# A new hand-written order of steps for a two-layer kernel (gated linear attention, then a leaky-ReLU feed-forward), on all engines and in the transfer queue

## The chip, the cores and the metric

One core of one Trainium2 chip runs the whole program. The metric is the device time of one execution in microseconds (us). The time of the kernel before the change is the median of three runs. One further execution was profiled; its trace is what the views below come from.

## The reference: what is computed

The inputs are q, k, v and f_logit, each of shape (4 batches, 8 heads, 768 steps, 48), and two weight matrices.

```
f = sigmoid(f_logit)
for t in range(768):
    state = f[t][:, None] * state + outer(k[t], v[t])      # per batch and head, 48 x 48
    y[t]  = q[t] @ state
x = y with heads side by side                               # 3072 tokens x 384
h = x @ w_in                                                # 384 -> 2048
out = maximum(0.01 * h, h) @ w_out                          # 2048 -> 384, float32
```

## The kernel before the change

The 768 steps are cut into six chunks of 128. The work is done in twelve units, numbered j = 0 to 11. Units 0 to 3 ("paired") take chunks 0 and 1 of one batch each; units 4 to 11 take one later chunk of two batches, two units for each chunk. Each unit yields 256 tokens, and the feed-forward part runs over these 256 tokens. Most steps exist twice for a unit, with a second number a = 0 or 1 (2 means both at once).

The program is one straight list of steps. Every step is a word in a long string called `order`; a word such as `dn_0_1_0@6` names a function, its numbers, and after the @ the PSUM banks that it writes. A loop at the end of the kernel (L659) splits each word and calls the function from a table called `parts`. The functions issue instructions to fixed engines, so the string at once sets the order in which each engine gets its work, and the order of the transfers, which all go through the queue of SyncE (SP in the profile). The engines run their own lists in order and wait for each other by semaphores.

The words, with the line at which their instructions show in the profile:

- **Transfers:** `Lf`, `Lk`, `Lq`, `Lv` load the inputs of a unit (384 KB for a paired unit at L158, two of 192 KB for a later one at L162). `WI_0` to `WI_4` load the pieces of w_in (L176; 384 KB for pieces 0 and 1, 768 KB for the other three) and `WO_0` to `WO_3` the quarters of w_out (768 KB, L181 and L184). The large pieces share three ring buffers, so WO_0 has to wait until piece WI_2 has been cast. `xk` and `xq` are transposing transfers of the scaled k and q for units 4 to 11 (L355), `ed` a small transfer of decays, `st` and `sh` store results.
- **Gates, on ScalarE (ACT):** `ge` and `gl` take an exponential and a logarithm of the gate (L236, L248); `cs` sums the logarithms over time on TensorE (L257 to L268); `dec` turns the sums into decays (L276 to L285).
- **Scaling:** `k` and `q` multiply by the decays (L301, on VectorE or GpSimd); for units 0 to 3 `tk` and `tq` transpose on TensorE (L335) and `ck`, `cq` copy the result out of PSUM (L348, L350).
- **Attention:** `sc` computes the scores (L371 for paired units, L378 for later ones), `mk` masks them on VectorE (L388, L392), `v` casts v (L307 to L316), `mx` and `ms` compute y (L409), `xt` copies it out as x (L469, L471). `pt`, `sf` and `sb` keep the running state (L482 to L508).
- **Feed-forward:** `cw` casts a half of a weight piece (L199 on ACT, L201 on VectorE or GpSimd). `up` is six matmuls of the first layer (L516) for a pair of 128-wide slices, `pr` the leaky ReLU on ACT (L521), `dn` four matmuls of the second layer (L528), `ob` the copy of the result out of PSUM. The last tile is done in two column halves, `dh`, `oh` and `sh` (L550 to L564).
- **Filling:** `id_n` issues matmuls of n times 128 columns on a constant tile (L207). Nothing reads their results; they keep TensorE busy where the list expects it to wait.

The last digit of `k`, `q`, `v`, `ck`, `cq`, `cw`, `xt`, `ob` and `sb` chooses the engine. Input buffers exist five times, PSUM has eight banks of 512 columns.

Of the kernel before, what the change touches and what calls it, by code (L numbers as in the profile page):

```python
# [15 lines left out]
def kernel(  # L16
# [587 lines left out]
    pr_1_3 WO_1 up_1_2@0 pr_1_0 Lf_3_2 cw_0_6_0 up_0_4@2 pr_1_2 cw_0_7_0 up_0_5@5 pr_0_4 WO_2 up_0_6@1 pr_0_5
    cw_1_0_0 cw_1_1_2 up_1_5@3 pr_0_6 up_1_7@4 pr_1_5 q_2_1_0 WO_3 up_1_4@6 pr_1_7 q_2_0_0 Lv_2_2 tq_2_1@7
    k_2_1_0 k_2_0_1 pr_1_4 Lq_3_2 dn_0_1_0@0 cq_2_1_0 Lf_4_1 tq_2_0@2 tk_2_1@5 Lf_4_0 cq_2_0_1 up_1_6@1 ck_2_1_0
    Lv_3_2 tk_2_0@3 cw_1_3_1 cw_1_2_2 dn_1_0_0@4 ck_2_0_0 pr_1_6 sc_2_1@6.7 sc_2_0@2.5 Lk_3_2 ge_3_0 mk_2_1_1
    dn_0_0_0@3 ge_3_1 mk_2_0_0 gl_3_0 dn_1_0_1 gl_3_1 mk_2_1_0 up_0_7@1 Lk_4_0 cw_1_4_1 cw_1_5_2 mk_2_0_1
    cs_3_0@7 pr_0_7 dn_0_1_1 dec_3_0 cs_3_1@2 Lf_5_1 cw_1_6_0 dn_0_0_1 dec_3_1 cw_1_7_0 dn_1_1_0@6 dn_0_0_2
    Lf_5_0 v_2_1_1 v_2_0_0 dn_1_1_1 dn_1_0_2 Lk_4_1 q_3_1_0 q_3_0_1 pt_2_2@5.1 mx_2_2@7.2 sf_2_0 Lv_4_1 dn_1_0_3  # L610
    xt_2_0_1 sb_2_0_1 tq_3_1@5 Lv_4_0 ge_4_2 sf_2_1 tq_3_0@7 dn_1_1_2 cq_3_1_0 sb_2_1_0 gl_4_2 ms_2 cq_3_0_0
    Lf_6_1 dn_1_1_3 ob_1_0_0 v_3_1_1 xt_2_1_0 dn_0_0_3 ob_1_1_1 Lf_6_0 k_3_1_0 k_3_0_1 v_3_0_1 cs_4_0@1 ob_0_0_0
    cs_4_1@5 dn_0_1_2 dec_4_0 Lq_4_0 tk_3_1@7 dn_0_1_3 dec_4_1 ck_3_1_0 Lq_4_1 tk_3_0@4 Lq_5_1 ge_5_2 ob_0_1_0
    up_2_0@2 ck_3_0_0 pt_3_2@6.3 pr_2_0 sc_3_0@1.7 sf_3_0 gl_5_2 Lk_5_0 sc_3_1@5.0 k_4_2_1 up_2_1@4 mk_3_1_0
    Lk_5_1 up_2_5@2 mk_3_0_1 pr_2_1 sb_3_0_0 up_2_2@6 mk_3_1_1 pr_2_5 Lq_5_0 up_2_4@5 v_4_2_0 mk_3_0_0 pr_2_2
    xk_4 sf_3_1 up_2_3@7 pr_2_4 dn_2_1_0@4 sb_3_1_1 pr_2_3 pt_4_1@0 ge_6_2 cs_5_1@2 cs_5_0@1 sf_4_1 up_2_7@6
    gl_6_2 sb_4_1_1 mx_3_2@3.5 q_4_2_1 pr_2_7 pt_4_0@7 xt_3_0_0 cs_6_0@0 dec_5_0 ms_3 sf_4_0 dn_2_0_0@6 xt_3_1_0
    cs_6_1@3 sb_4_0_0 dn_2_1_1 xq_4 dec_5_1 dn_2_0_1 k_5_2_0 st_0_1 up_3_3@7 dec_6_1 q_5_2_1 dn_2_1_2 pr_3_3
    up_2_6@5 dec_6_0 up_3_2@1 xq_5 pr_2_6 up_3_1@2 pr_3_2 up_3_0@3 pr_3_1 xk_5 dn_2_1_3 pr_3_0 up_3_7@7 Lv_5_0
    up_3_5@0 Lv_5_1 pr_3_7 ob_2_1_0 sc_4_2@5.1.2.3 Lf_7_0 pr_3_5 dn_3_0_0@7 Lf_7_1 mk_4_1_1 st_0_0 dn_2_0_2  # L620
    mk_4_0_1 ed_5 dn_3_0_1 mk_4_1_0 Lk_6_1 mk_4_0_0 dn_2_0_3 dn_3_1_0@4 Lk_6_0 up_3_4@0 Lv_6_1 sc_5_2@3.1.2.5
    pr_3_4 dn_3_1_1 Lv_6_0 v_5_2_0 mk_5_1_1 up_3_6@0 mk_5_0_1 st_1_1 dn_3_0_2 mk_5_1_0 pr_3_6 mk_5_0_0
    mx_4_2@5.1 st_1_0 ge_7_2 Lq_6_1 mx_5_2@2.0 gl_7_2 xt_4_1_0 Lf_8_1 xt_4_0_0 ob_2_0_1 pt_5_1@3 pt_5_0@1
    xt_5_0_1 dn_3_1_2 sf_5_1 Lf_8_0 xt_5_1_1 sf_5_0 up_4_0@5 sb_5_1_0 Lq_6_0 dn_3_0_3 sb_5_0_1 pr_4_0 cs_7_0@6
    cs_7_1@2 Lv_7_1 dn_3_1_3 dec_7_0 k_6_2_0 up_5_5@3 Lv_7_0 v_6_2_0 up_4_1@0 Lq_7_0 ob_3_1_0 pr_5_5 Lq_7_1
    ob_3_0_0 up_4_2@1 dec_7_1 up_5_0@5 Lk_7_0 pt_6_0@6 pt_6_1@4 up_5_1@3 sf_6_0 pr_4_1 Lk_7_1 pr_5_0 sf_6_1
    up_5_3@7 pr_5_1 xk_6 sb_6_0_1 dn_4_0_0@2 sb_6_1_0 pr_4_2 pr_5_3 up_5_2@0 q_6_2_0 ge_8_2 dn_5_1_0@6 pr_5_2
    up_4_7@5 gl_8_2 up_5_4@4 v_7_2_0 xq_6 pr_4_7 up_4_3@3 pr_5_4 cs_8_0@1 pr_4_3 st_3_1 cs_8_1@7 dn_4_1_0@0
# [5 lines left out]
    mk_7_1_0 gl_9_2 Lq_9_0 up_6_4@2 sf_7_0 ob_5_0_1 mx_7_2@6.1 ob_4_1_0 Lq_9_1 pr_6_1 sb_7_0_0 sf_7_1 pr_6_4
    up_6_5@4 xt_7_0_1 xt_7_1_0 sb_7_1_0 up_6_7@5 k_8_2_0 pr_6_5 up_7_5@0 pr_6_7 v_8_2_0 up_7_6@3 pr_7_5 up_6_0@2
    pr_7_6 q_8_2_0 cs_9_1@7 cs_9_0@6 pr_6_0 up_7_0@1 dec_9_1 dn_6_0_0@4 xq_8 up_7_4@5 pr_7_0 up_7_1@0 pr_7_4
    xk_8 dn_6_1_0@3 pr_7_1 up_7_2@2 dec_9_0 Lf_10_1 k_9_2_1 dn_7_1_0@7 Lf_10_0 q_9_2_0 up_6_6@1 st_5_1 pr_7_2
    up_7_3@5 pr_6_6 dn_7_0_0@0 pr_7_3 xq_9 up_7_7@6 dn_7_1_1 pr_7_7 st_5_0 up_6_3@2 xk_9 dn_7_0_1 pr_6_3
    dn_7_1_2 Lv_9_0 ge_10_2 sc_8_2@1.5.6.2 Lv_9_1 dn_7_0_2 st_4_0 mk_8_0_1 gl_10_2 Lf_11_1 dn_7_1_3 mk_8_1_0
    ed_9 pt_8_1@5 mk_8_1_1 dn_7_0_3 ob_7_1_1 Lf_11_0 sf_8_1 dn_6_1_1 ob_7_0_1 st_4_1 mk_8_0_0 sb_8_1_0 dn_6_0_1  # L640
    dn_6_1_2 dn_6_0_2 Lq_10_1 dn_6_1_3 mx_8_2@6.2 Lq_10_0 sc_9_2@7.5.0.1 xt_8_1_1 xt_8_0_0 Lk_10_1 v_9_2_0
    dn_6_0_3 mk_9_0_0 Lk_10_0 cs_10_0@2 mk_9_1_0 pt_8_0@6 up_8_0@7 dec_10_0 Lq_11_1 sf_8_0 up_8_3@0 Lq_11_0
    ob_6_0_1 mk_9_1_1 sb_8_0_0 pr_8_0 Lk_11_1 cs_10_1@2 pt_9_0@6 mk_9_0_1 pt_9_1@4 pr_8_3 Lk_11_0 up_8_1@1
    sf_9_1 dec_10_1 up_8_4@7 ob_6_1_0 Lv_10_1 sb_9_1_0 pr_8_1 up_8_2@5 sf_9_0 ge_11_2 Lv_10_0 dn_8_0_0@0
    q_10_2_0 pr_8_4 sb_9_0_0 up_8_6@4 gl_11_2 st_6_0 mx_9_2@2.3 pr_8_6 xq_10 pr_8_2 cs_11_0@1 xt_9_0_0 cs_11_1@6
    k_10_2_1 dn_8_1_0@7 dec_11_0 xt_9_1_0 dn_8_0_1 dec_11_1 dn_8_1_1 xk_10 q_11_2_1 up_8_5@4 up_9_4@5 pr_8_5
    up_8_7@2 pr_9_4 xq_11 k_11_2_1 dn_8_0_2 pr_8_7 up_9_0@3 st_7_0 dn_8_0_3 pr_9_0 xk_11 v_10_2_0 dn_8_1_2
    ob_8_0_0 up_9_1@1 st_7_1 Lv_11_1 up_9_3@6 pr_9_1 Lv_11_0 up_9_2@4 pr_9_3 st_6_1 dn_9_1_0@5 pr_9_2 dn_9_0_0@2
    up_9_7@3 st_8_0 up_9_5@0 pr_9_7 dn_9_0_1 pr_9_5 up_9_6@1 sc_10_2@6.4.3.0 pr_9_6 dn_9_1_1 mk_10_1_0 dn_9_0_2
    mk_10_0_1 dn_9_1_2 mk_10_1_1 mk_10_0_0 dn_9_0_3 dn_9_1_3 ob_9_0_0 mx_10_2@1.3 ob_9_1_0 sc_11_2@4.0.6.2  # L650
    xt_10_1_1 xt_10_0_0 v_11_2_0 dn_8_1_3 mk_11_1_0 up_10_4@5 mk_11_1_1 ob_8_1_1 up_10_6@1 mk_11_0_1 st_8_1
    pr_10_4 st_9_1 mk_11_0_0 up_10_0@3 pr_10_6 st_9_0 up_10_1@6 pr_10_0 up_10_2@2 pr_10_1 up_10_3@7 pr_10_2
    up_10_7@0 pr_10_3 mx_11_2@5.4 pr_10_7 dn_10_1_0@1 xt_11_0_1 xt_11_1_0 up_10_5@3 dn_10_1_1 pr_10_5 up_11_6@6
# [39 lines left out]
```

## Time and profile before

| | |
|---|---|
| time, median of 3 runs (lowest to highest) | 178.56 us (177.96 to 178.77) |
| the profiled execution, time and span | 178.35 us and 176.6 us |
| TensorE busy (PE) | 170.0 us, 96% of the span |
| ScalarE, VectorE, GpSimd busy | 119.7, 89.3 and 55.9 us |
| transfers | 34.44 MB, mean 195 GB/s |

The span runs from the first to the last instruction that the profile shows; the time has 1.75 us around it. PE is TensorE's matmuls, PEld its weight loads, DVE is VectorE, POOL is GpSimd, and SPq is the queue of SyncE that issues the transfers. In the groups, the columns are line, engine, operation, output and inputs, shapes, count, then busy time in us and the mean of one in ns, then the engine's idle time before these instructions and what ended it.

### The profile page before, as it was taken

How to read it: one execution, taken by the hardware profiler on the slowest of the kernel's cores; microseconds unless marked ns; L12 is line 12 of the kernel's file. 1: busy time of each engine (PE TensorE's matmuls, PEld its weight loads, DVE VectorE, ACT ScalarE, POOL GpSimd, SP SyncE). 2: the span in 40 equal slices, each digit the busy share in tenths (PEclk: the TensorE clock that was granted, in tenths of full speed). 3: DMA queues.
4: the chain of work that ended last, by engine and by line, in shares of the span. 5: the costliest groups of instructions: out<-in, count | busy, mean ns of one | idle time of the engine just before them, and what ended most of it. 6: DMA issues, size and time to landing. Idle time of an engine off the chain costs nothing.

```text
span 176.6 us, 5545 instructions
## 1 busy us (share of the span) xinstructions
PE 170.0 (96%) x2295; PEld 129.7 (73%) x2295; DVE 89.3 (51%) x194; ACT 119.7 (68%) x244; POOL 55.9 (32%) x103
## 2 busy tenths in 40 slices
...
GB/s 139 282 301 262 344 341 339 388 296 219 185 198 193 166 182 162 171 214 206 169 203 207 213 182 183 189 242 205 190 170 208 196 222 112 137 4 0 0 71 111
DMA packets 106856, 34.44 MB, mean 195 GB/s; under 512 B 101072, under 2 KB 105040, under 8 KB 106832
## 3 DMA queue, kind: packets, MB, share of 16 engines
...
## 4 chain that ended last, share of the span: by engine, by line
PE 71%; SPq 14%; DMA 10%; POOL 1%; issue 1%; DVE 1%; ACT 0%; DVEq 0%
PE ps L516 30%; PE ps L528 29%; SPq L158 9%; PE ps L409 5%; DMA ring<-in_moe_w_in_dram 4%; DMA k_raw<-in_k_dram 3%; DMA ring<-in_moe_w_out_dram 3%; SPq L162 3%; SPq L176 3%; PE ps L378 3%; PE ps L550 2%; PE ps L265 1%; PE ps L487 1%; POOL w_out L201 1%; ACT w_in L199 0%
## 5 line engine op out<-in xcount | busy, mean ns | idle before, releaser
L516 PE MATMUL ps<-xT,w_in 128*128 128x256 bf16 x576 | 70.0, 273 | 0.7 <-ACT w_in L199 0.7
L521 ACT ACTIVATE gT<-ps 128x512 bf16<-128x512 f32 x96 | 55.6, 610 | 21.6 <-PE ps L516 19.3
L528 PE MATMUL ps<-w_out,gT 128*128 128x384 bf16 x368 | 68.4, 326 | 0.0
L516 PEld LDWEIGHTS <-w_in 128*128 128x128 bf16 x576 | 60.8, 110 | 6.2 <-ACT w_in L199 0.9
L528 PEld LDWEIGHTS <-gT 128*128 128x128 bf16 x368 | 34.2, 98 | 19.1
L392 DVE TENSOR_TENSOR wm<-ps,ut 128x512 bf16<-128x512 f32 x32 | 20.1, 684 | 14.0 <-ACT gT L521 8.0
L307 POOL CAST vb<-v_raw 128x768 bf16<-128x768 f32 (+1 forms) x11 | 8.1, 738 | 31.7 <-DMA v_raw<-in_v_dram 29.1
L505 POOL TENSOR_TENSOR sf<-sf,end 128x192 f32<-128x192 f32 x12 | 6.9, 571 | 31.3 <-DVE sf L499 27.5
L301 POOL TENSOR_TENSOR kh<-k_raw,em 128x768 bf16<-128x768 f32 (+1 forms) x8 | 11.7, 1458 | 12.8 <-DMA k_raw<-in_k_dram 6.7
L301 DVE TENSOR_TENSOR qh<-q_raw,at 128x384 bf16<-128x384 f32 (+1 forms) x11 | 9.2, 845 | 11.4 <-DMA q_raw<-in_q_dram 7.8
L574 DVE COPY osb<-ps 128x384 f32<-128x384 f32 x12 | 6.6, 556 | 15.0 <-PE ps L528 13.5
L276 ACT ACTIVATE em<-ps 128x384 bf16<-128x384 f32 x24 | 12.1, 503 | 2.0 <-PE ps L265 1.2
L469 ACT CAST xT<-ps 128x384 bf16<-128x384 f32 x11 | 5.6, 534 | 11.1 <-PE ps L409 11.0
L236 ACT ACTIVATE f_raw<-f_raw 128x384 f32<-128x384 f32 (+1 forms) x16 | 10.8, 689 | 3.1 <-DMA f_raw<-in_f_logit_dram 2.9
L508 POOL CAST sb<-sf 64x192 bf16<-64x192 f32 x30 | 11.3, 376 | 3.6 <-DVE sf L497 1.9
L471 DVE CAST xT<-ps 128x384 bf16<-128x384 f32 x13 | 7.2, 567 | 10.1 <-PE ps L409 10.0
L277 ACT ACTIVATE at<-ps 128x384 bf16<-128x384 f32 x24 | 12.2, 508 | 0.0
L499 DVE TENSOR_TENSOR sf<-sf,ps 64x192 f32<-64x192 f32 x32 | 11.2, 351 | 0.7
L207 PE MATMUL ps<-warm 128*128 128x512 bf16 (+3 forms) x31 | 10.2, 441 | 1.1 <-DVE warm L83 1.1
L388 DVE TENSOR_TENSOR wm<-ps,pair_mask 128x512 bf16<-128x512 f32 x16 | 10.1, 686 | 1.9 <-PE ps L371 1.8
L248 ACT ACTIVATE lf<-f_raw 128x384 bf16<-128x384 f32 (+1 forms) x16 | 10.7, 687 | 0.2
L572 ACT COPY osb<-ps 128x384 f32<-128x384 f32 x11 | 5.3, 479 | 8.1 <-PE ps L528 8.0
...
## 6 DMA issues: line engine op xcount, KB each, us to landing
...
```

The costliest lines, as they stand in the source:

```text
L158: nc.sync.dma_start(out=by_pair(raw(j, x))[:, h].rearrange("t h s d -> t h (s d)"), in_=srcs[x][j, h, 0:2 * C, :].rearrange("h (t s) d -> ...
L236: nc.scalar.activation(gates(j)[:, part], gates(j)[:, part], AF.Exp, scale=-1.0)
L248: nc.scalar.activation(dst, src, AF.Ln, bias=1.0)
L276: nc.scalar.activation(ems[j % 2][:, a], t[:, 0:H * D], AF.Exp, scale=1.0)
L277: nc.scalar.activation(ats[j % 2][:, a], t[:, 0:H * D], AF.Exp, scale=-1.0)
L301: eng.tensor_mul(heads(j, to[j % NR], a)[:, :, :, 0:D], raw_heads(j, x, a), decays(j, by, a))
L392: nc.vector.tensor_mul(w, src.rearrange("t (p n) -> t p n", p=P2), ut[:, None, :].to_broadcast([128, P2, 128]))
L499: nc.vector.tensor_add(sf[rows], sf[rows], new)
L508: eng.tensor_copy(out=sb[rows, :, y * D:y * D + D], in_=sf[rows])
L516: nc.tensor.matmul(pm[:, i, :], w_in_of(ff, kk), xTs[j % 3][:, kk].rearrange("t a s -> t (a s)"), start=(kk == 0), stop=(kk == NK - 1))
L521: nc.scalar.activation(gTs[j % 3][:, 2 * g:2 * g + 2, :], pm, AF.Prelu, alpha=0.01)
L528: nc.tensor.matmul(po, gTs[j % 3][:, ff, 128 * a:128 * a + 128], w_out_b[quarter][:, ff % 4, :], start=(ff == 0), stop=(ff == NF - 1))
```

## The change

Only the string `order` changes. Apart from the filling and the digit that chooses an engine, the same steps are there, each once. TensorE's list, the lists of the other engines and the list of transfers are all in a new order, and many PSUM banks are others. The filling goes from 112 times 128 columns in twelve places to 102 in nine. Some copies, casts and scalings go to another engine: ACT copies 9 `xt` and 9 `ob` in place of 11 and 11, and 5 `ck` in place of 2, VectorE the others; the casts of weights are 6 on ACT, 4 on VectorE and 6 on GpSimd in place of 4, 7 and 5.

Among the transfers, Lf_2 and Lv_1 come before WI_1, Lk_2 comes before WO_0, and Lk_3 comes before WO_3, Lq_3, Lv_3 and the two Lf_4. Lf_7 comes before unit 5's transposes and Lf_6 after unit 4's; Lk_7 and Lv_7 come after unit 6's transposes. The core of the diff (the stretches up to the first steps of unit 2, around the scores of unit 6, and the end):

```
-    Lf_0_0 Lf_0_1 Lq_0_1 Lk_0_1 Lk_0_0 Lq_0_0 ge_0_0 Lv_0_2 ge_0_1 Lf_1_2 gl_0_1 Lk_1_2 gl_0_0 id_40@6 cs_0_1@0
-    Lq_1_2 cs_0_0@1 WI_1 dec_0_1 Lv_1_2 k_0_1_0 dec_0_0 q_0_1_0 Lf_2_2 id_16@6 tk_0_1@2 k_0_0_0 ck_0_1_1 id_4@6
-    tq_0_1@3 WI_0 q_0_0_0 cq_0_1_1 id_3@6 tk_0_0@4 ck_0_0_0 id_3@0 tq_0_0@5 sc_0_1@6.7 WI_2 v_0_1_0 cq_0_0_1
-    mk_0_1_0 v_0_0_1 id_5@2 sc_0_0@0.1 mk_0_1_1 id_3@4 pt_0_2@2.3 mk_0_0_0 WI_3 ge_1_0 sf_0_0 gl_1_0 mk_0_0_1
-    ge_1_1 sb_0_0_0 id_16@5 cs_1_0@4 WI_4 gl_1_1 dec_1_0 id_5@6 cs_1_1@5 k_1_0_0 mx_0_2@6.7 dec_1_1 tk_1_0@0
-    q_1_0_0 ms_0 xt_0_0_1 ck_1_0_0 q_1_1_1 tq_1_0@2 xt_0_1_1 sf_0_1 cw_0_1_1 k_1_1_1 cq_1_0_0 id_6@4 tq_1_1@1
-    cq_1_1_0 id_8@6 tk_1_1@4 v_1_0_1 v_1_1_0 sc_1_0@5.0 ck_1_1_1 mk_1_0_0 sb_0_1_0 id_3@3 pt_1_2@6.7 ge_2_1
-    mk_1_0_1 sc_1_1@3.2 ge_2_0 up_0_1@1 sf_1_0 gl_2_1 cw_0_0_2 gl_2_0 cs_2_1@4 mk_1_1_1 pr_0_1 cs_2_0@5 sb_1_0_0
-    mk_1_1_0 dec_2_1 up_0_0@0 mx_1_2@6.2 cw_0_2_1 cw_0_3_0 ms_1 sf_1_1 xt_1_0_1 up_0_3@1 WO_0 pr_0_0 xt_1_1_0
...
-    up_4_4@1 pr_5_7 up_4_5@7 pr_4_4 xq_7 up_5_6@4 pr_4_5 dn_5_0_1 pr_5_6 Lf_9_1 dn_4_1_1 Lf_9_0 dn_5_1_3 ed_7
-    sc_6_2@3.1.7.4 ob_5_1_0 dn_4_0_2 Lk_8_1 mk_6_1_0 st_3_0 dn_5_0_2 mk_6_0_0 st_2_1 Lv_8_1 dn_4_0_3 mk_6_1_1
...
-    dh_11_1_0@7 dn_10_0_2 oh_11_1_0_1 sh_11_1_0 dn_11_0_2 st_10_1 dn_10_0_3 dn_11_0_3 ob_10_0_1 dh_11_1_1
-    st_10_0 ob_11_0_1 st_11_0 oh_11_1_1_0 sh_11_1_1
+    Lf_0_1 Lf_0_0 Lq_0_1 Lk_0_1 Lk_0_0 ge_0_1 Lq_0_0 gl_0_1 ge_0_0 id_30@6 cs_0_1@0 gl_0_0 dec_0_1 cs_0_0@1
+    Lv_0_2 Lf_1_2 dec_0_0 q_0_1_0 Lf_2_2 k_0_1_0 k_0_0_1 id_26@6 tk_0_1@2 Lk_1_2 tq_0_1@3 ck_0_1_1 q_0_0_0
+    id_5@6 tk_0_0@4 cq_0_1_1 ck_0_0_0 Lq_1_2 id_5@0 tq_0_0@5 sc_0_1@6.7 v_0_1_1 v_0_0_0 cq_0_0_0 mk_0_1_0 id_2@2
+    sc_0_0@0.1 Lv_1_2 pt_0_2@2.3 mk_0_0_1 ge_1_0 mk_0_1_1 ge_1_1 gl_1_0 WI_1 sf_0_0 gl_1_1 id_16@5 cs_1_0@4
+    mk_0_0_0 ge_2_0 sb_0_0_0 cs_1_1@5 ge_2_1 mx_0_2@6.1 gl_2_0 sf_0_1 gl_2_1 cs_2_0@7 dec_1_1 ms_0 WI_0 cs_2_1@2
+    dec_1_0 k_1_1_0 k_1_0_0 WI_2 id_5@3 tk_1_1@0 dec_2_1 q_1_1_0 ck_1_1_1 q_1_0_0 WI_3 tq_1_1@3 tk_1_0@5 v_1_1_1
+    v_1_0_0 cq_1_1_0 tq_1_0@4 xt_0_1_0 sc_1_1@2.0 WI_4 xt_0_0_1 pt_1_2@3.1 mk_1_1_1 cq_1_0_1 cw_0_1_2 ck_1_0_1
+    mk_1_1_0 Lk_2_2 dec_2_0 sc_1_0@6.4 cw_0_0_2 sf_1_0 up_0_1@0 mk_1_0_1 sb_1_0_0 up_0_0@5 mk_1_0_0 pr_0_1
+    sb_0_1_0 sf_1_1 pr_0_0 id_1@7 mx_1_2@2.3 cw_0_3_1 cw_0_2_0 sb_1_1_0 id_12@4 ms_1 xt_1_0_0 WO_0 up_0_3@7
...
+    cs_8_1@7 pr_5_6 dn_5_0_0@5 xq_7 dec_8_1 cs_8_0@6 k_7_2_1 dn_5_0_1 dec_8_0 sc_6_2@1.3.0.4 st_3_0 up_5_7@7
...
+    up_11_5@7 pr_11_4 up_11_6@1 pr_11_5 dn_10_0_2 pr_11_6 dn_11_0_1 dh_11_1_0@2 dn_10_0_3 oh_11_1_0_1 sh_11_1_0
+    dn_10_1_2 ob_10_0_0 dn_11_0_2 st_10_0 dn_10_1_3 dn_11_0_3 ob_10_1_0 dh_11_1_1 st_10_1 ob_11_0_1 st_11_0
+    oh_11_1_1_0 sh_11_1_1
```

More of the change, by code (lines that the diff above doesn't have):

```diff
@@ L604 @@
[L604 to L628, printed above, removed]
@@ L634 @@
[L634 to L653, printed above, removed]
@@ new lines @@
+    mk_1_1_0 Lk_2_2 dec_2_0 sc_1_0@6.4 cw_0_0_2 sf_1_0 up_0_1@0 mk_1_0_1 sb_1_0_0 up_0_0@5 mk_1_0_0 pr_0_1
+    sb_0_1_0 sf_1_1 pr_0_0 id_1@7 mx_1_2@2.3 cw_0_3_1 cw_0_2_0 sb_1_1_0 id_12@4 ms_1 xt_1_0_0 WO_0 up_0_3@7
+    xt_1_1_1 Lf_3_2 up_0_2@4 pr_0_3 cw_0_5_0 up_1_2@0 cw_0_4_1 up_1_3@6 pr_0_2 Lq_2_2 pr_1_2 up_1_1@5 cw_0_7_2
+    pr_1_3 up_1_4@1 pr_1_1 up_1_0@2 cw_0_6_1 up_0_5@3 pr_1_4 WO_1 pr_1_0 k_2_1_0 k_2_0_1 up_0_4@7 pr_0_5
+    tk_2_1@4 up_0_6@0 Lv_2_2 ck_2_1_0 cw_1_1_0 cw_1_0_2 up_1_6@6 pr_0_6 tk_2_0@5 WO_2 pr_1_6 up_1_5@1 ck_2_0_0
@@ new lines @@
+    ge_3_1 up_0_7@2 ge_3_0 Lk_3_2 gl_3_1 dn_1_0_0@3 gl_3_0 q_2_0_0 q_2_1_1 pr_1_5 dn_1_1_0@4 pr_0_7 tq_2_0@0
+    dn_0_1_0@6 pr_0_4 cq_2_0_0 WO_3 cs_3_1@5 cw_1_2_1 cw_1_3_0 tq_2_1@1 dn_0_0_0@2 dec_3_1 cq_2_1_0 Lq_3_2
+    dn_1_0_1 v_2_1_0 v_2_0_1 sc_2_0@0.7 sc_2_1@1.5 mk_2_0_1 dn_0_0_1 Lv_3_2 mk_2_1_0 cs_3_0@7 cw_1_5_1 cw_1_4_2
+    dn_0_1_1 mk_2_1_1 dec_3_0 mk_2_0_0 dn_1_1_1 dn_0_1_2 Lf_5_0 k_3_1_0 k_3_0_1 up_1_7@1 dn_1_1_2 pr_1_7 Lf_5_1
+    pt_2_2@5.7 cw_1_6_1 cw_1_7_2 mx_2_2@0.1 sf_2_0 dn_0_0_2 Lf_4_0 xt_2_0_1 sb_2_0_1 tk_3_0@5 q_3_0_0 tk_3_1@0
@@ new lines @@
+    ck_3_0_1 dn_1_1_3 q_3_1_0 Lf_4_1 sf_2_1 v_3_1_1 v_3_0_0 dn_0_1_3 Lv_4_0 ob_1_1_0 ck_3_1_1 tq_3_0@5 sb_2_1_0
+    tq_3_1@7 ob_0_1_0 cq_3_0_1 dn_1_0_2 cq_3_1_0 Lv_4_1 dn_0_0_3 ge_5_2 dn_1_0_3 ob_0_0_0 gl_5_2 ms_2 Lq_4_0
+    pt_3_2@4.0 xt_2_1_0 ob_1_0_1 sc_3_0@6.5 sf_3_0 Lk_4_1 sc_3_1@7.2 up_2_5@1 ge_4_2 mk_3_1_1 sb_3_0_0 Lk_4_0
+    up_2_1@3 mk_3_1_0 pr_2_5 up_2_2@4 gl_4_2 mk_3_0_1 Lq_4_1 up_2_3@2 sf_3_1 pr_2_1 v_4_2_0 pr_2_2 mk_3_0_0
+    up_2_0@1 Lf_7_1 pr_2_3 sb_3_1_1 cs_4_1@7 pr_2_0 cs_4_0@5 Lf_7_0 cs_5_1@3 dec_4_1 up_2_6@0 mx_3_2@4.6 pr_2_6
@@ new lines @@
+    cs_5_0@2 Lq_5_1 dec_4_0 xt_3_0_0 ms_3 dn_2_0_0@1 xt_3_1_0 dec_5_1 Lq_5_0 k_4_2_0 up_2_7@7 q_4_2_1 up_2_4@0
+    Lk_5_1 pr_2_7 dn_2_1_0@4 pr_2_4 st_0_1 pt_4_0@5 pt_4_1@6 ge_7_2 dn_2_0_1 sf_4_0 Lk_5_0 dec_5_0 sf_4_1
+    dn_2_1_1 sb_4_0_0 up_3_5@3 sb_4_1_1 dn_2_1_2 xk_4 pr_3_5 q_5_2_1 up_3_7@7 gl_7_2 dn_2_1_3 xq_4 pr_3_7
+    dn_2_0_2 ob_2_1_0 up_3_1@0 Lf_6_1 k_5_2_0 Lf_6_0 up_3_0@5 pr_3_1 xq_5 up_3_2@6 pr_3_0 up_3_3@2 pr_3_2 xk_5
+    dn_3_1_0@3 pr_3_3 up_3_4@7 st_0_0 dn_2_0_3 pr_3_4 Lv_5_0 sc_4_2@4.0.5.6 ge_6_2 dn_3_1_1 mk_4_0_0 Lv_5_1
```

39 lines of the change are left out of this document (33 added, 6 removed).

## The prediction

> **What bounds the kernel now.** I read TensorE's waits first, then its busy time by stage, then the chain that ended last where it leaves TensorE, then ACT's and SP's own rows there.
>
> ```profile
> PE ps L516 <- ACT w_in L199: 0.7, 1, 0.7
> PE ps L335 <- DVE kh L301: 0.7, 1, 0.7
> ```
> ```profile
> 22.80:47.00 24.20, 24.18 (x318) 18.82 (x318) 13.97 (x30) 20.44 (x47) 9.75 (x15) 1.00 1.01 302
> 47.00:48.00 1.00, 0.35 (x6) 0.34 (x6) 0.95 (x2) 1.00 (x5) 0.81 (x1) 1.00 0.44 90
> 48.00:173.20 125.20, 125.20 (x1604) 98.29 (x1601) 57.09 (x108) 80.47 (x152) 35.81 (x54) 1.00 0.78 165
> ```
>
> In the windows the first number after the stretch is its length, the next TensorE's busy time; the last two are the transfer engines' share and GB/s. From 22.8 us on TensorE is idle once, for 0.65 us at 47 us. A busy matmul may still be a slow one, so the rate is read from the chain, which counts from issue to issue:
>
> ```profile
> 48.06 0.65 PE ps L528 x4
> 48.72 0.22 PE ps L335 x4
> 48.94 0.66 PE ps L516 x6
> ```
>
> An `up` takes 0.66 us, a `dn` 0.65, a `tk` or `tq` 0.22; the windows say that TensorE goes on like this, and an order can't make these steps cheaper. So the time has three parts: a start, until the first `up` of the big weight pieces (up_0_3, at 22.8 us); 150.4 us of TensorE's list, with 0.65 us of idle time in it; and an end, 3.4 us from 173.2 to 176.6.
>
> **The start.** I compared the lists as sets. Ahead of up_0_3 TensorE has the same steps in both orders, filling apart, and ahead of WI_2 in the transfer queue stand the same fourteen transfers. So neither the work left at that point nor the bytes ahead of WI_2 change.
>
> ```profile
> 15.55 6.37 DMA ring<-in_moe_w_in_dram
> 21.91 0.02 issue
> 21.94 0.84 ACT w_in L199
> ```
>
> WI_2 lands at 21.92, its cast on ACT takes 0.84, and up_0_3 starts. That landing ends the start; if it comes at the same time again, what is shuffled ahead of it costs nothing as long as it is done sooner. This cover has to be worked out, for ACT gets four operations (the two `ge_2` and two `gl_2`) ahead of dec_1.
>
> ```profile
> 16.73 0.51 ACT L307 CAST vb<-v_raw 128x384 bf16<-128x384 f32 x1 [0.21 <-DMA v_raw<-in_v_dram]
> 17.14 0.39 ACT L313 CAST v<-v_raw 128x64 bf16<-128x64 f32 x2
> 17.43 0.58 ACT L348 COPY kT<-ps 128x512 bf16<-128x512 bf16 x1
> 17.92 0.94 ACT L236 ACTIVATE f_raw<-f_raw 128x384 f32<-128x384 f32 x2
> 18.77 0.93 ACT L248 ACTIVATE lf<-f_raw 128x384 bf16<-128x384 f32 x2
> 19.59 0.58 ACT L521 ACTIVATE gT<-ps 128x512 bf16<-128x512 f32 x1
> 20.07 0.48 ACT L276 ACTIVATE em<-ps 128x384 bf16<-128x384 f32 x1
> 20.44 0.49 ACT L277 ACTIVATE at<-ps 128x384 bf16<-128x384 f32 x1
> 20.81 0.18 ACT L279 ACTIVATE end<-ps 128x4 f32<-128x4 f32 x1
> ```
> ```profile
> L388 DVE TENSOR_TENSOR wm<-ps,pair_mask 128x512 bf16<-128x512 f32 x16 | 10.1, 686 | 1.9 <-PE ps L371 1.8
> ```
> ```profile
> L499 DVE TENSOR_TENSOR sf<-sf,ps 64x192 f32<-64x192 f32 x32 | 11.2, 351 | 0.7
> ```
>
> From start to start, a `v` on ACT takes 0.7 us (16.73 to 17.43), a copy 0.49 (to 17.92), the four gate operations of a unit 1.7 (to 19.59), a `pr` 0.48, a `dec` 0.9. Lf_1 stays eighth in the queue and Lf_2 is now ninth, so ACT can take the gates of units 1 and 2 one after the other, from 10.3 us, when it takes those of unit 1 before:
>
> ```profile
> 10.26 0.52 ACT L236 ACTIVATE f_raw<-f_raw 128x384 f32<-128x384 f32 x1
> ```
>
> Its new list: both sets of gates to 13.7, dec_1_1, dec_1_0 and dec_2_1 to 16.4, v_1_1 and four copies (ck_1_1, xt_0_0, cq_1_0, ck_1_0; 0.7 + 2.0) to 19.1. Now sc_1_0 can start; up_0_1 follows from 19.5 to 20.1 and up_0_0 to 20.8. VectorE does the last two masks of unit 1 and the two halves of sf_1_1 (2 x 0.69 + 2 x 0.35 = 2.1 us) from about 19.7 to 21.8. mx_1 follows the masks at 21.1 and ends near 21.8, then come 12 times 128 columns of filling and ms_1; ACT finishes pr_0_0 near 21.4. Both engines are free for the casts of WI_2 just as it lands, with 0.1 us to spare on VectorE and 0.5 on ACT. So up_0_3 starts between 22.8 and 23.3; I take 22.9, near the lower end, as the landing alone sets that. **Cost: 0.1 us**; the bounds are 0 and 0.5, and a gain is left to a rival.
>
> Filling falls by 10 times 128 columns. That gains nothing, as TensorE waits for WI_2 whether it is filled or not. WI_1 moves behind Lf_2 and Lv_1, 768 KB, or 2.6 us at the 302 GB/s of the second window; up_0_1, its first reader, now stands behind sc_1_0, which hides that.
>
> **The gap at 47 us.**
>
> ```profile
> 40.98 6.05 DMA k_raw<-in_k_dram
> 47.03 0.02 issue
> 47.05 0.57 DVE kh L301
> ```
> ```profile
> 47.19 1.19 POOL L301 TENSOR_TENSOR kh<-k_raw,em 128x384 bf16<-128x384 f32 x1 [2.13 <-DMA k_raw<-in_k_dram]
> ```
>
> The k of unit 3 lands at 47.03, VectorE scales half of it in 0.57 us, and TensorE's tk_3_1, ready 0.65 us before, starts. In the new queue Lk_3 passes WO_3 (768 KB), Lq_3, Lv_3 (384 KB each) and both Lf_4 (192 KB each): 1920 KB, 6.5 us at 302 GB/s. On TensorE the first tk_3 moves forward too, past four `dn` (2.6 us), two tq (0.4), ms_2 and two cs_4 (taken at up to 0.8 together): it would be ready between 43.2 and 44.0. k_3 lands near 40.5, GpSimd, which now scales that half, takes 1.2: 41.7, at least 1.5 us early. The gap goes. **Gain: 0.65 us.** What Lk_3 passes lands 1.3 us later. Lk_2 moves ahead of WO_0, and WO_0 lands at most 1.3 us later, near 29.6 (28.4, the start of its casts before, plus 1.3); its casts take up to 1.2, and its first reader dn_1_0_0 stands behind thirteen `up` and two tk, at 22.9 + 8.6 + 0.4 = 31.9: covered by 1.1 us. Without that cover each transfer of 384 KB costs 1.3. Next late on TensorE's side are short reuses of a bank: cs_3_0 takes that of sc_2_0 with a score and a `dn` between (about 0.95 us, for a mask of 0.69), tk_3_1 that of mx_2 with a `dn` and a tk between (0.87 us, for a copy of about 0.5). They fit, by some 0.3 us.
>
> **Later units.** What is late next is read where TensorE's list jumps forward: sc_6, the scores of unit 6, passes six `dn` and one `up`, 6 x 0.65 + 0.66 = 4.6 us. Its operands come from the transfers xk_6 and xq_6.
>
> ```profile
> 80.71 2.01 SPq L162 DMA_DIRECT2D v_raw<-in_v_dram  x2
> 82.77 1.78 SPq L162 DMA_DIRECT2D q_raw<-in_q_dram  x2
> 84.59 3.44 SPq L162 DMA_DIRECT2D k_raw<-in_k_dram  x2
> 88.15 1.82 SPq L355 DMA_TRANSPOSE kT<-kh  x1
> 90.08 1.24 SPq L355 DMA_TRANSPOSE qT<-qh  x1
> ```
> ```profile
> DMA to landing us min/median/max: 3.1/3.1/3.1
> ```
> ```profile
> 94.96 0.55 PE ps L378 x16
> ```
>
> xq_6 lands at 93.2 (90.08 + 3.1) and sc_6 starts at 94.96: 1.8 us of slack. In the new queue Lk_7 and Lv_7, four loads, no longer stand ahead of it, and ed_7 does. Six loads took from 80.71 to 88.15, 1.24 us each; less some 0.4 for ed_7 (an estimate: it moves a few KB), xq_6 lands 4.6 us sooner, at 88.6. sc_6 would start at 94.96 - 0.65 + 0.1 - 4.6 = 89.8. Slack 1.2 us: I take no stall, but there is less room than before.
>
> **End.** Both lists close with a `dn`, the last `dh`, its copy and its store: 0.
>
> **Sum.** Against the profiled execution's own 178.35 us (176.6 of span, 1.75 around it): + 0.1 - 0.65 = 177.8. That execution lay 0.2 under the median of 178.56; from the median the sum is 178.0. I forecast 177.9.
>
> **A. As above** (0.42): 177.9, give or take 0.4 for the bounds of the start.
>
> **B. The start shortens** (0.18). Loads share their engines with blocks of instructions.
>
> ```profile
> DMA  5969999999999999999999999999732210002589
> ```
> ```profile
> q8 instruction: 1, 0.02, 0.5%
> ```
>
> This is 42 to 48 us in 40 slices, in tenths busy, and the one large packet of instructions in it. From about 46.3 to 47.4 the sixteen engines stand nearly empty while k_3 has not landed, as if one that had the block lagged behind the rest. If a block falls elsewhere in the new order, WI_2 can land up to 1.1 us sooner; VectorE, free at 21.8, then holds up_0_3 to 22.5, 0.4 less than in A: 177.5. Against it: the same steps stand ahead of up_0_3, so blocks should come at like times. The Trainium skill (Runtime: NRT & Kernel Launch, Instruction fetch mechanics) says that crossing a block costs one tail bump, mostly hidden; by that rule B gains nothing. The stretch above speaks against the rule where a load is waited for.
>
> **C. TensorE's clock comes later** (0.12).
>
> ```profile
> 1.06 4.45 PE L207 MATMUL ps<-warm 128*128 128x512 bf16 x10 [1.06 <-DVE warm L83]
> 5.30 0.37 PE L257 MATMUL ps<-lf,bu 128*128 128x192 bf16 x1
> ```
> ```profile
> 6.35 1.02 PE L207 MATMUL ps<-warm 128*128 128x512 bf16 x4
> 7.24 0.40 PE L335 MATMUL ps<-ident,kh 128*128 128x128 bf16 x4
> ```
>
> Ten fills took 4.24 us to the next step, 0.42 each; four later ones 0.22 each, though the windows' granted clock reads 1.00. The first filling shrinks from 40 times 128 columns to 30, so it ends near 4.3, and a gap can follow. If full rate then comes late, id_26 (6.5 such matmuls) costs 1.3 us more and unit 0 slides by that; ACT's 0.5 of margin takes part: 0.8 more, 178.7. The Trainium skill (TensorE: Matmul & The Clock Gate, Part 1) has the array start throttled and released after about 3.4 us of sustained work, in free-running windows; by that rule less filling risks this. Against it: the first gate loaded is now the first one used, so unit 0's sums are ready sooner and fill the gap.
>
> **D. Unit 6's transposes are late** (0.28), the case on the other side. xq_6 gains its 4.6 us only if the queue sets its issue. If SP waits for k_6 and q_6 to be scaled on VectorE, whose list has the masks of unit 5 ahead of them, the gain can be anything down to nothing. From a gain under 3.4 us on sc_6 waits, and every step behind it in TensorE's list. With no gain the stall is 3.4 us, 181.3; I take 1.9, somewhat past the middle: 179.8. For it: sc_10 jumps forward in the same way, past five `dn`. Against it: the rows above show loads issued without a pause.
>
> **How the numbers follow.** A measurement of this kernel can tell about 0.5% from no change: 177.67 and 179.45 are the bounds. A gives 0.14 faster and 0.28 same; B 0.16 and 0.02; C 0.12 same; D 0.04 same and 0.24 slower. Faster 0.30, same 0.46, slower 0.24. The range, 177.0 to 180.2, takes in A, B, C and two thirds of D; A's own is 177.5 to 178.3.
>
> **What would show it.** Right: one wait of TensorE for w_in near 22 us, none for kh at 47, only busy time from up_0_3 to the end, and 149.8 us from up_0_3 to the last matmul. Wrong: a wait of L378 for kT or qT (D); up_0_3 before 22.6 (B), or after 23.3 with slow fills past 6 us (C); new idle time between 23 and 60 us, from a `cw` or a bank.

## The result, and the profile after

The kernel after took 178.87 us (median of 20 executions, 177.42 to 180.12), the kernel before, run beside it, 178.59 (20 executions, 177.36 to 180.85). The ratio is 1.0, with a 95% interval of 0.9974 to 1.0026: no difference that the measurement can tell. A second comparison (in the experiments) gave 0.9964 (0.9935 to 0.9993), a gain of a third of a per cent. Of the 20 executions of after, six show a mean granted clock of TensorE of 0.988 to 0.990 and took 179.74 us in the median, the other fourteen 178.27. The forecast was 177.9, likeliest no change.

The profiled execution of after took 178.26 us, with a span of 176.5. First its page, the lines of the span and of the engines' busy time:

```profile
span 176.5 us, 5544 instructions
PE 169.4 (96%) x2294; PEld 129.9 (74%) x2294; DVE 95.8 (54%) x199; ACT 120.0 (68%) x242; POOL 54.3 (31%) x100
```

Against 176.6 us and 170.0 of PE before, little seems to have happened. The waits of TensorE say otherwise (line that waited, who released it, total, times, longest):

```profile
PE ps L207 <- DVE warm L83: 1.1, 1, 1.1
PE ps L371 <- ACT kT L348: 0.9, 1, 0.9
PE ps L257 <- ACT lf L248: 0.7, 2, 0.4
PE ps L335 <- DVE qh L301: 0.5, 1, 0.5
PE ps L516 <- POOL w_in L201: 0.2, 1, 0.2
```

The wait of 0.65 us for k at 47 us is gone, and so is the wait of L516 for WI_2 (the cast on ACT) at 22 us. All waits left lie ahead of 21 us. For the first, the tile k_raw between 25 and 45 us, and TensorE's timeline:

```profile
L158 SPq DMA_DIRECT2D k_raw<-in_k_dram x1: 538/538/538, 30.4 to 30.4; - x1
DMA to landing us min/median/max: 8.2/8.2/8.2
```
```profile
43.51 0.61 PE L335 MATMUL ps<-ident,kh 128*128 128x128 bf16 x8
```

Lk_3 is issued at 30.4 and lands at 38.6; tk_3 starts at 43.51 without a wait. The last matmuls in the chain that ended last, before and then after (start, duration):

```profile
171.88 1.33 PE ps L550 x16
```
```profile
171.97 1.33 PE ps L550 x16
```

TensorE ends at 173.21 and 173.30. So what was won at 47 us was lost elsewhere, and it was lost ahead of up_0_3. The chain of after from 20 to 24 us:

```profile
19.57 0.84 POOL w_in L201
20.41 0.05 issue
20.45 0.83 PE ps L516 x6
21.28 0.06 PE ps L207
21.34 0.71 PE ps L409 x58
22.05 0.09 issue
22.14 0.29 PE ps L409 x4
22.42 0.75 PE ps L207 x3
23.18 0.28 PE ps L409 x12
23.46 1.43 PE ps L516 x12
```

Read downward: the cast of WI_0 ends, up_0_0 runs, mx_1 runs, stops before its last four matmuls and takes 1.08 us by the timeline (21.27 to 22.35), then come three filling matmuls (id_12), ms_1, and up_0_3. Before, the chain here was WI_2's landing and its cast. The cast of WI_2 no longer sets anything:

```profile
22.11 0.83 ACT L199 CAST w_in<-ring 128x768 bf16<-128x768 f32 x1 [0.19 <-DMA ring<-in_moe_w_in_dram]
23.39 0.84 PE L516 MATMUL ps<-xT,w_in 128*128 128x256 bf16 x6
```

It is done at 22.94, and up_0_3 starts at 23.39 in TensorE's timeline, 22.82 before: 0.57 later. From up_0_3 to the end of the last matmul it is 173.21 - 22.82 = 150.39 us before and 173.30 - 23.39 = 149.91 after: 0.48 shorter. The two nearly cancel, + 0.09. (0.65 of waiting went and the stretch is 0.48 shorter; the other 0.17 was not traced to a step.)

### The profile page after: what moved, and what is told of

Same layout as the page of the kernel before. It is cut to its first block, busy times and chain, and to the rows that moved or that the text cites. A ratio compares the mean times of both kernels' runs of the same rounds, so it can differ in the third digit from the quotient of the medians.

```text
span 176.5 us, 5544 instructions
## 1 busy us (share of the span) xinstructions
PE 169.4 (96%) x2294; PEld 129.9 (74%) x2294; DVE 95.8 (54%) x199; ACT 120.0 (68%) x242; POOL 54.3 (31%) x100
## 4 chain that ended last, share of the span: by engine, by line
PE 87%; SPq 6%; DMA 4%; POOL 1%; issue 1%; DVE 0%; DVEq 0%; POOLq 0%
PE ps L516 36%; PE ps L528 35%; PE ps L409 6%; SPq L158 6%; DMA part<-in_moe_w_in_dram 4%; PE ps L378 3%; PE ps L265 2%; PE ps L550 2%; PE ps L487 1%; PE ps L335 1%; POOL w_in L201 1%; PE ps L371 1%; PE ps L482 1%; PE ps L207 0%; PE ps L268 0%
## 5 line engine op out<-in xcount | busy, mean ns | idle before, releaser
L516 PE MATMUL ps<-xT,w_in 128*128 128x256 bf16 x576 | 68.9, 273 | 0.4 <-POOL w_in L201 0.2
L528 PE MATMUL ps<-w_out,gT 128*128 128x384 bf16 x368 | 67.1, 326 | 0.0
L516 PEld LDWEIGHTS <-w_in 128*128 128x128 bf16 x576 | 60.6, 110 | 5.3 <-POOL w_in L201 0.8
L528 PEld LDWEIGHTS <-gT 128*128 128x128 bf16 x368 | 34.5, 98 | 19.6
L392 DVE TENSOR_TENSOR wm<-ps,ut 128x512 bf16<-128x512 f32 x32 | 20.0, 684 | 22.1 <-PE ps L378 13.7
L307 POOL CAST vb<-v_raw 128x768 bf16<-128x768 f32 (+1 forms) x12 | 9.1, 762 | 35.1 <-DMA v_raw<-in_v_dram 33.7
L574 DVE COPY osb<-ps 128x384 f32<-128x384 f32 x14 | 7.7, 556 | 20.0 <-PE ps L528 19.1
L301 POOL TENSOR_TENSOR qh<-q_raw,at 128x768 bf16<-128x768 f32 (+1 forms) x6 | 9.2, 1527 | 17.6 <-DMA q_raw<-in_q_dram 9.7
L471 DVE CAST xT<-ps 128x384 bf16<-128x384 f32 x15 | 8.3, 568 | 10.1 <-PE ps L409 10.0
L301 POOL TENSOR_TENSOR kh<-k_raw,em 128x384 bf16<-128x384 f32 (+1 forms) x6 | 8.2, 1362 | 12.7 <-ACT at L277 5.2
L301 DVE TENSOR_TENSOR kh<-k_raw,em 128x384 bf16<-128x384 f32 (+1 forms) x10 | 8.9, 892 | 5.4 <-DMA k_raw<-in_k_dram 4.3
L508 POOL CAST sb<-sf 64x192 bf16<-64x192 f32 x26 | 9.8, 377 | 6.0 <-DVE sf L497 4.5
L207 PE MATMUL ps<-warm 128*128 128x512 bf16 (+2 forms) x30 | 8.6, 411 | 1.1 <-DVE warm L83 1.1
```

The lines of the kernel that those rows point to most:

```text
L301: eng.tensor_mul(heads(j, to[j % NR], a)[:, :, :, 0:D], raw_heads(j, x, a), decays(j, by, a))
L392: nc.vector.tensor_mul(w, src.rearrange("t (p n) -> t p n", p=P2), ut[:, None, :].to_broadcast([128, P2, 128]))
L516: nc.tensor.matmul(pm[:, i, :], w_in_of(ff, kk), xTs[j % 3][:, kk].rearrange("t a s -> t (a s)"), start=(kk == 0), stop=(kk == NK - 1))
L528: nc.tensor.matmul(po, gTs[j % 3][:, ff, 128 * a:128 * a + 128], w_out_b[quarter][:, ff % 4, :], start=(ff == 0), stop=(ff == NF - 1))
```

## The experiments

**One part alone, in the kernel before.** Is the earlier transfer enough to take the wait at 47 us away?

```
-    ... q_2_1_0 WO_3 ... sc_2_0@2.5 Lk_3_2 ge_3_0
+    ... q_2_1_0 Lk_3_2 WO_3 ... sc_2_0@2.5 ge_3_0
```

> The kernel before with one word moved: Lk_3 ahead of WO_3, as in the changed kernel. Theory (the place in the queue alone made the gap at 47 us): no wait of TensorE for kh at 47 us, up_0_3 still at 22.8, 0.65 us less of span: 175.9 to 176.0. Rival (an instruction block at 44.5 us delays whatever load is awaited then): 0.3 us or more of TensorE's idle time between 40 and 50 us at another step, and 0.3 us or less gained.

It took 178.96 us (12 executions), 1.0033 times the kernel before (1.0004 to 1.0062). Two of its waits of TensorE:

```profile
PE ps L482 <- POOL vb L307: 0.6, 1, 0.6
PE ps L265 <- DVE xT L471: 0.5, 1, 0.5
```

L335 no longer waits for k, but pt_2 (L482) now waits 0.6 us for v_2, at 41.9 us, because Lk_3 had also passed Lv_2: the cast of v_2 began at 41.31 here and at 40.00 in the kernel before, 1.3 us later. The second wait, for a copy of x, is at 59.1 us; what made it was not followed up. The wait went to the next load that had no room. The expectation of a gain was wrong. The rival had named idle time of 0.3 us or more at another step between 40 and 50 us, and that came; its cause, the block of instructions, did not: here the block was in the queues from 44.8 to 45.8 us, behind the wait. That the move pays in the kernel after because other words moved along (Lv_2 ahead of WO_2, TensorE's list around unit 3) fits, but no run undid those words.

**That part undone, in the kernel after.** Lk_3 stands just ahead of k_3_1_0.

```
-    ge_3_1 up_0_7@2 ge_3_0 Lk_3_2 gl_3_1 ...
+    ge_3_1 up_0_7@2 ge_3_0 gl_3_1 ...
-    Lf_5_0 k_3_1_0 ...
+    Lf_5_0 Lk_3_2 k_3_1_0 ...
```

> The changed kernel with Lk_3 moved back behind WO_3, Lq_3, Lv_3 and Lf_5_0, just ahead of the step that reads it. Theory: k_3 lands at 43.6 in place of 38.6, GpSimd scales the first half in 1.2, the transpose tk_3_0 starts at 44.9 in place of 43.5, and the span grows by 1.3 us, since TensorE has no idle time later to give it back. Rival (idle time early is given back later): the span grows by under 0.5 us.

One execution took 182.21 us, with a span of 180.4, 3.9 more than the kernel after where 1.3 was expected. The longest of TensorE's waits, a row of its timeline, and the window from the wait on (length, busy time of each engine, then the granted clock of TensorE ahead of the last two columns):

```profile
PE ps L335 <- POOL kh L301: 2.2, 1, 2.2
```
```profile
46.97 2.55 PE L528 MATMUL ps<-w_out,gT 128*128 128x384 bf16 x8
```
```profile
46.14:49.20 3.06, 3.06 (x16) 1.86 (x17) 2.91 (x7) 1.77 (x5) 2.31 (x5) 0.50 0.86 172
```

The place is right: the wait at tk_3 is back, 2.2 us long. The size has two parts more. Behind the pause TensorE ran at half rate for 3 us (granted 0.50; eight `dn` matmuls took 2.55 us, against 1.47 for eight in the kernel before), which is some 1.5 us, and in this execution up_0_3 came 0.3 us later. Hardly anything was given back: the last matmul came 3.9 us later than in the kernel after. The Trainium skill (TensorE: Matmul & The Clock Gate, Part 1) says that the array falls to half rate after an idle window of about 3.4 us; here a pause of 2.2 us was enough.

**The side on which the forecast feared a loss.** The loads of unit 7 go back ahead of unit 6's transposes.

```
-    xk_6 ... xq_6 ... q_7_2_0 Lk_7_0 up_5_0@1 ge_8_2 Lk_7_1 ... ge_9_2 Lv_7_1 mk_6_0_0 dn_4_1_3 gl_9_2 Lv_7_0
+    Lk_7_0 Lk_7_1 Lv_7_1 Lv_7_0 xk_6 ... xq_6 ... q_7_2_0 up_5_0@1 ge_8_2 ... ge_9_2 mk_6_0_0 dn_4_1_3 gl_9_2
```

> The changed kernel with Lk_7 and Lv_7, four loads, put back ahead of unit 6's transposing transfers. Theory (the queue sets when xq_6 lands, the price of case D): xq_6 lands 3.7 to 4.6 us later, at 92.5 to 93.4, sc_6 waits from 90.4 for it and the span grows by 2.1 to 3.0 us to 178.6 to 179.5. Rival (SP waits for the scaling on VectorE anyway): xq_6 lands less than 2 us later and the span grows by under 0.4 us.

One execution took 180.24 us, with a span of 178.4, 1.9 more than the kernel after. The theory had 2.1 to 3.0; in this execution up_0_3 began 0.3 earlier, so 2.2 were lost behind it. The wait that it named is there:

```profile
92.31 0.62 PE L378 MATMUL ps<-qT,kT 48*128 48x128 bf16 x16 [2.05 <-DMA qT<-qh]
```

In the kernel after, SP's timeline, the tile qT between 84 and 88.5 us and TensorE's timeline show the same step in time:

```profile
84.51 1.28 SPq L355 DMA_TRANSPOSE qT<-qh  x1
```
```profile
DMA to landing us min/median/max: 4.3/4.3/4.3
```
```profile
90.41 0.62 PE L378 MATMUL ps<-qT,kT 48*128 48x128 bf16 x16
```

xq_6 lands at 84.51 + 4.3 = 88.8, 1.6 us ahead of sc_6. TensorE's list needs those loads out of the way, and in the kernel after they are.

**The start: the filling left out.** `id_12@4` is taken out of the kernel after.

> The changed kernel without the 12 times 128 columns of filling between mx_1 and ms_1. Theory F (the filling itself holds ms_1, and so up_0_3, back): ms_1 starts when mx_1 ends, and up_0_3 at 22.9 to 23.1 us, just after the casts of WI_2 at 22.95, in place of 23.4; the span falls by 0.35 to 0.5 us to about 176.1. Theory G (the later landing of WI_0 and WI_2 sets the start, the filling only fills): up_0_3 stays near 23.4 with 0.4 us or more of idle time ahead of it, and the span stays at 176.5.

It took 177.62 us (12 executions), 0.9942 times the kernel before (0.9904 to 0.998). TensorE's timeline, two rows of it:

```profile
22.45 6.08 PE L516 MATMUL ps<-xT,w_in 128*128 128x256 bf16 x54 [0.50 <-ACT w_in L199]
29.00 0.40 PE L335 MATMUL ps<-ident,kh 128*128 128x128 bf16 x4 [0.47 <-DVE kh L301]
```

up_0_3 again waits for WI_2's cast and starts at 22.45, 0.94 earlier than in after, as theory F had it. Part of that is luck of this execution: WI_2's cast began at 21.56 here, at 22.11 there, 0.55 later; by that the filling's own share is about 0.4. The second row is new: k_2 landed 1.1 us later than in after, with a block of instructions in the queues from 26.1 to 27.1 (25.1 to 26.1 there), and tk_2 waits 0.5.

**The filling doubled** (`id_12@4` to `id_24@4`).

> The kernel after, with the filling between mx_1 and ms_1 doubled (id_12 to id_24: six matmuls of 128x512 in place of three, which took 0.75 us). Theory F (the filling stands on the path to up_0_3, because mx_1 ends only when WI_2's cast is nearly done): up_0_3 begins about 0.75 us later than in the kernel after, near 24.2 us, and the median rises by about as much, to 179.6. Rival G (up_0_3 is set by WI_2's landing and cast, the filling only stands beside them): up_0_3 stays within 0.2 us of the cast's end and the median within 0.3 of the kernel after.

It took 178.46 us (11 executions, 177.59 to 181.4), ratio 0.9987 (0.9944 to 1.003): theory F's 0.75 did not show in the median. The profiled execution was the longest of them, 181.4 us, and shows why its own time is no measure:

```profile
23.21 0.28 PE L409 MATMUL ps<-wm,v 64*32 64x128 bf16 x4 [1.70 <-issue]
23.43 2.68 PE L207 MATMUL ps<-warm 128*128 128x512 bf16 x6
```

The stop before the last four matmuls of mx_1 is 1.7 us here, ended by nothing that the profile shows, and the six filling matmuls behind it took 0.45 us each, half rate again.

**No filling at all** (every `id_` word taken out).

> The kernel after without any filling matmul (all words id_ dropped; no output hangs on them). Theory F (the fillings of the start stand beside waits, save the last, which stands on the path): up_0_3 comes 0.5 to 1.0 us earlier as without id_12 alone, the median is near 177.7. Rival C' (the fillings bring TensorE to its full rate, and without them the matmuls of the first 20 us run at half rate for longer): the matmuls of 128x128 and 128x192 before 10 us take about twice as long, up_0_3 comes 0.5 us or more later than in the kernel after, and the median is 179.3 or more.

It took 178.65 us (10 executions, 177.34 to 179.96), ratio 1.0006 (0.9963 to 1.0049): neither the gain of F (177.7) nor clearly the loss of C' (179.3 or more), which the upper end of the interval just takes in. Both have something in the trace:

```profile
7.42 0.61 PE L335 MATMUL ps<-ident,kh 128*128 128x128 bf16 x4 [1.06 <-DVE kh L301]
22.38 6.06 PE L516 MATMUL ps<-xT,w_in 128*128 128x256 bf16 x54 [0.36 <-DVE w_in L201]
```

The four transposes at 7.4 us took 0.61 us, 0.39 in the kernel after, so half rate lasted longer, though the granted clock of the windows reads 1.00 there; but up_0_3 begins at 22.38, since it waits for the cast of WI_2 here too.

**Filling of two other sizes, and the kernel after once more, on one chip.**

> The kernel after with one filling matmul of 128x512 between mx_1 and ms_1 in place of three (id_12 to id_4: 0.25 us in place of 0.75). Theory F (the filling stands on the path): up_0_3 comes 0.45 us earlier than in the kernel after run beside it, and the median falls by 0.4 to 0.5. Rival S (the time goes with the pause of TensorE ahead of the last four matmuls of mx_1, which ended 1.4 us behind the end of a 16-KB instruction packet in four traces so far): the filling hardly matters, the median falls by at most 0.2, and a trace with the pause has it again ending 1.4 us behind that packet.

> The kernel after with nine filling matmuls between mx_1 and ms_1 in place of three (id_12 to id_36: 2.25 us in place of 0.75). Theory F: up_0_3 comes 1.5 us later, the median 1.5 above that of the kernel after beside it. Rival G (in most executions mx_1 ends early enough for some 0.75 of filling more to lie beside the cast of WI_2, as the six matmuls of id_24 left the median where it was): up_0_3 comes 0.7 to 0.8 later, the median as much.

> The kernel after once more, unchanged, for a second profiled execution beside the other two. Theory S: where the 16-KB instruction packet of about 20 us ends by 20.0, mx_1 runs without a pause and up_0_3 begins at 22.9 or earlier; where it ends later, the pause ends 1.4 us behind it. Rival: the pause of 0.3 us comes again whatever that packet does. The median stays within 0.5 of 178.9.

Of 12 executions each: 178.13 us with id_4 (ratio 0.9963, 0.993 to 0.9996), 178.07 with id_12, the kernel after (0.9964, 0.9935 to 0.9993), 179.05 with id_36 (1.0015, 0.999 to 1.004). Smaller filling gained nothing in the median, where F expected 0.45; larger filling cost 0.98, where F expected 1.5 and G 0.75. So here about two thirds of an added length are paid, and the first columns may be free; the median of id_24 above showed no cost at all. The traces show when. The chain of the kernel after in this second execution:

```profile
19.87 0.84 POOL w_in L201
...
21.64 0.74 PE ps L409 x61
22.38 0.75 PE ps L207 x3
23.13 0.28 PE ps L409 x12
23.41 1.43 PE ps L516 x12
```

mx_1 takes 0.74 us here, without a stop, and yet up_0_3 comes at 23.41, as in the first (23.46). From the start of WI_0's cast to up_0_3 this list of TensorE needs 0.84 + 0.05 + 0.83 + 0.06 + 0.74 + 0.75 + 0.28 = 3.55 us; from the start of WI_2's cast the other way needs 0.84. The filling is free only where WI_2's cast starts at least 3.55 - 0.84 = 2.7 us behind WI_0's. (That is the sum where up_0_0 waits for WI_0's cast, as in these two traces.) It was 22.11 - 19.57 = 2.5 behind in the first trace of after and 22.11 - 19.87 = 2.2 in the second: the list set the start. With id_4 the list needs 0.5 less, and WI_2's cast came 3.3 behind: TensorE waited for it.

```profile
18.15 0.83 POOL L201 CAST w_in<-part 128x768 bf16<-128x768 f32 x1 [0.30 <-DMA part<-in_moe_w_in_dram]
21.46 0.83 ACT L199 CAST w_in<-ring 128x768 bf16<-128x768 f32 x1 [0.46 <-DMA ring<-in_moe_w_in_dram]
22.40 6.06 PE L516 MATMUL ps<-xT,w_in 128*128 128x256 bf16 x54 [0.55 <-ACT w_in L199]
```

With id_36 up_0_3 began at 24.94, and the stop in mx_1 was back (chain):

```profile
21.69 0.71 issue
22.39 0.29 PE ps L409 x4
```

**The stop in mx_1.** Every trace holds one large packet of instructions (16 KB, queue q8) near 20 us; in a window cut around it the list of queues has

```profile
q8 instruction: 1, 0.02, 6.0%
```

Its end, from such windows, against the start of the last four matmuls of mx_1, and the time from the first matmul of mx_1 to the next step, from TensorE's timeline:

```
kernel                     packet ends   the four start   mx_1 takes
after                      20.7          22.14            1.08
after, Lk_3 late           21.0          22.42            1.41
after, loads 7 early       20.4          21.85            1.38
id_24                      21.7          23.21            2.70
id_36                      21.2          22.39            1.70
after, second trace        20.2          22.1             0.74
id_12 left out             18.9          21.4             0.74
id_12 left out, Lk_2 early 20.1          21.4             0.74
id_4                       19.0          21.0             0.74
```

In the five traces with a stop it ends 1.2 to 1.5 us behind the packet, always before the same four matmuls; in the others TensorE got there 1.3 to 2.5 us behind it. The kernel before has a trace of the same thing at another step of its list. Counted from the first matmul of the program, the stop always lies ahead of the 352nd. In the kernel before that is the eighth from the end of mx_1, and there TensorE pauses about 0.1 us and goes on at 21.56, 1.5 us behind its packet (20.1). The row that holds it lasts 0.51, where it lasts 0.39 without a stop:

```profile
21.36 0.51 PE L409 MATMUL ps<-wm,v 64*32 64x128 bf16 x16
```

With the same list and the packet done by 19.0 (Lk_3 early in the kernel before) there is no such pause. Without any filling the 352nd is one of the `up`, reached at 23.6, 1.8 us behind its packet, and nothing stops. So the place goes with the number of matmuls issued and not with the step, and the moment with the packet. This bears theory S (in the expectation for id_4) out as far as timing can: TensorE had run out of instructions. That the filling hardly matters, its other half, holds for id_4 and not for id_36. No run moved the packet alone, so the cause is inferred, not switched.

**The lowest median.** id_12 left out, and Lk_2 one place earlier, ahead of WI_4, for the wait of tk_2 seen above.

> The kernel after without id_12, and with Lk_2 one place earlier in the queue (ahead of WI_4). Without id_12 alone tk_2 waited 0.5 us for k_2, which landed at 28.36; WI_4 landed at 25.62 and its halves of w_in are first read at 30.8. Theory: k_2 lands about 1 us earlier, near 27.3, the wait of 0.5 goes, and the median comes 0.5 us below that of id_12 left out alone, near 177.2. Rival: the casts of WI_4, now 1.0 to 1.1 us later, hold up the activations that are queued behind them on ScalarE, TensorE then waits for a free bank or for gT, and the median stays near 177.6.

It took 177.44 us (12 executions, 176.83 to 178.94), 0.9956 times the kernel before (0.9921 to 0.9991):

```profile
22.32 6.06 PE L516 MATMUL ps<-xT,w_in 128*128 128x256 bf16 x54 [0.41 <-ACT w_in L199]
```

tk_2 starts at 28.21 without a wait, and the later casts of WI_4 hold nothing up. The 0.5 expected came to 0.18 between two medians that overlap; with id_4 k_2 was in time without the move, so the wait is not in every execution. Both versions that leave out id_12 alone or with this move beat the kernel before, by 0.4 and 0.6%; neither is separated from the kernel after by its second comparison.

## Why the prediction was right, and where it was not

**The time and the sign.** No change was the likeliest case and came out, and 178.87 lies in the range. The middle, 177.9, was a little low: 0.55 us of gain was summed; the first comparison gave none, the second 0.43 (between the medians) to 0.64 (by the ratio). In the two profiled executions the sum's terms came out as - 0.48 and + 0.57, so the whole gain was lost to one term. That the time still lies in the range owes something to its width of 3.2 us.

**Gap at 47 us: right.** It was to go, for 0.65. k_3 landed at 38.6 (predicted 40.5), tk_3 was ready at 43.5 (43.2 to 44.0), the stretch behind up_0_3 takes 149.9 (149.8), with no wait of TensorE in it: 0.48 gained. Late Lk_3 brings the wait back, so that word is needed; the same word alone in the kernel before moves the wait to v_2, so it is not enough.

**Start: the term that was mis-sized.** It was + 0.1, up_0_3 at 22.9 within 22.8 to 23.3; two traces show 23.39 and 23.34, + 0.5 to + 0.6. The step that failed is the one that set the filling at nothing, "TensorE waits for WI_2 whether it is filled or not". That had been read from before, where WI_2 was the last to come. In the new list mx_1 ends near 22.3, because WI_0's cast comes at 19.6 to 19.9 (19.06 before) and, in one trace, because of the stop in it; three filling matmuls then stand between it and ms_1. The margin that should have been worked out was that of TensorE's own list against WI_2, not only those of VectorE and ScalarE. The prediction's own figures would have shown that there was none: mx_1 ending near 21.8, three fills of 0.22 and 0.28 for ms_1 make 22.7, level with the 22.8 at which WI_2's cast was to be done. So of its signs the wait for w_in near 22 us failed to come.

**B, blocks of instructions: did not occur in after, half of it in other traces.** In the two traces of after WI_2 landed at 22.1 and 21.9, as before (21.9). In seven of the eight other traces of its variants it landed 0.4 to 1.8 us sooner, and in the four of these where id_12 was left out or cut to id_4, up_0_3 began at 22.3 to 22.45, the 22.5 of B; with id_12 or more the list held it at 23.1 or later. That a moved block brought WI_2 sooner is not shown. Blocks moved, by up to 1 us and more, and by the timing a load and TensorE were late by it: k_2 with id_12 left out, mx_1 in five traces. The Trainium skill (Runtime: NRT & Kernel Launch, Instruction fetch mechanics) calls the crossing of a block mostly hidden; of the traces here five show TensorE stopped behind one, with mx_1 longer by 0.3 to 2.0 us.

**C, the clock: did not occur.** In the profiled execution full rate came sooner, not later. TensorE's timeline of after near 4.5 us:

```profile
4.50 0.32 PE L257 MATMUL ps<-lf,bu 128*128 128x192 bf16 x1
...
4.77 0.25 PE L257 MATMUL ps<-lf,bu 128*128 128x192 bf16 x1
...
6.04 1.56 PE L207 MATMUL ps<-warm 128*128 128x512 bf16 x7
```

From 4.77 on a matmul of 192 columns shows 0.25 instead of 0.32, and the fill at 6.04 takes 0.22 for each, where before the fill at 6.35 was the first at that rate. The gates of unit 0 followed the first filling within 0.1 us, as was said against C. But the moment is not set by the list alone: with the same start of the list, full rate was there by 4.5 us in three other traces and only near 6.2 in two (id_24, and loads 7 early). Even there id_26, which C had at half rate, took 0.1 us more at most.

**D, unit 6's transposes: right to doubt, did not occur.** xq_6 landed at 88.8 (predicted 88.6) and sc_6 has 1.6 us of room (1.2). SP was not held up by the scaling. The loads back in front made the execution 1.9 us longer, as much as D was priced at, but that is a coincidence: there the queue itself was late, and D had SP wait for the scaling.
